# Two strip transposes of the first batch held behind loads of the second batch's v, in a fused attention and mixer kernel

## The chip, the cores and the metric

The kernel runs on one core of one Trainium2 chip. The metric is the device time of one execution in microseconds, as the median of several runs. A profile of one more execution shows what each engine did: PE (TensorE), DVE (VectorE), ACT (ScalarE), POOL (GpSimd) and SP (SyncE, which here only issues DMAs).

## The reference

There are 8 batches of 3136 rows. An attention without softmax is gated by `u`, and a mixer with a low-rank term and two channel matrices follows.

```python
scores = (1.0 / S) * np.matmul(z, z.transpose(0, 2, 1))      # z: 8 x 3136 x 64
attn = np.maximum(scores, 0.0) ** 2
x = u * np.matmul(attn, v)                                   # u, v: 8 x 3136 x 256
h = x.transpose(0, 2, 1) @ U @ V                             # U: 3136 x 32, V: 32 x 3136
y = x + h.transpose(0, 2, 1)
out = y + np.maximum(y @ w_ch1, 0.0) @ w_ch2                 # 256 -> 1024 -> 256
```

## The kernel before

Every order is written out by hand: each engine runs its instructions in the order in which the program names them, and the scheduler moves nothing.

**Tiles.** The 3136 rows of a batch are 25 tiles of 128, numbered 0 to 24, of which the last is half full. The attention matrix is symmetric, so for each row tile `j` only 13 of the 25 blocks are computed: the panel `A[j]` holds the blocks (j, j) to (j, j+12), counted round the 25. PE multiplies the parts of z into PSUM (L359), ACT applies the ReLU and the scale (L372), DVE squares (L374). The 12 blocks that are missing for output `o` are the mirror images of blocks that lie in `A[o]`: one DMA transpose of `A[o][:, 128:]` writes them into a tile called a strip (function `turn`, L394). A strip is 128 x 12 x 128 in bf16, and its DMA is issued by SP. The pool holds seven strips. Output `o` is the sum over 25 blocks times v (function `half`, L472), 13 from panels and 12 from its strip. Outputs are accumulated in pairs; `close_pair` takes a pair out of PSUM (L486, L487), multiplies it by u (L502) and so frees the pair's tile of u. As the last step of the first output of a pair, block 24 of both outputs is taken together, which reads the strips of both.

**Order of the first batch.** Outputs are taken in the order 12, 13, ..., 24, 0, ..., 11. "Output 4" and "output 8" in that order are blocks 16 (`LEAD`) and 20 (`LEAD + NG`); the text calls their strips strip 16 and strip 20. `start_up` does outputs 12 to 15, then 16 to 19 together, since little of A exists yet; it calls `turn` for the strips 16, 17, 18, 19, 20, 21 and 22 in this order. The main loop starts with output 20 (`attend_steps`), whose list `js` says in which order its blocks are taken: for output 20 five blocks from panels, then its strip, then the other eight panel blocks. Strips 23, 24, 0 and so on follow from the main loop. SP issues the transposes in this order, and a transpose that waits holds all that follow it.

**The loads.** POOL issues the loads of v, u, z and the weights in program order, and the few POOL instructions between them wait in the same line. v of the next batch comes in nine pieces: `V_PARTS` is (0,3), (3,6), (6,9), (9,12), (12,15) and so on in tiles, of 192 KB each in SBUF. `start_up` issues the pieces 0 to 2 of batch 1 behind the loads of the first weight matrix, U and V (L306). Pieces 3 and 4 are issued later, behind a one-column copy on POOL from strip 19 into a tile `mark` that nothing reads (L869): the copy makes POOL wait until strip 19 has landed. Then come the loads of u for outputs 20 and 22 (L456), each of which also waits until DVE has freed its buffer, and the two halves of the last, short piece of v (L309).

Of the kernel before, what the change touches and what calls it, by code (L numbers as in the profile page):

```python
# [42 lines left out]
def kernel(  # L43
# [11 lines left out]
    nc = tc.nc  # L55

    B, S, D = u.shape
# [13 lines left out]
    NB = HALF + 1  # L71
    FIRST = HALF
    AHEAD = 4
    LEAD = FIRST + AHEAD
    NG = 4
# [20 lines left out]
    mark = persist.tile([P, 1], BF16, name="mark")  # L96
# [29 lines left out]
    v_both = [persist.tile([P, NT, D], BF16, name=f"v{k}") for k in range(2)]  # L126
# [5 lines left out]
    def turns(i):  # L132
        return (FIRST + i) % NT
# [168 lines left out]
    def load_v(b, part):  # L302
        t0, t1 = part
        v_bf = v_both[b % 2]
        if t0 < NF:
            pool_dma(out=v_bf[:, t0:t1, :], in_=rows(v[b])[:, t0:t1, :])  # L306
        else:
            for r in halves:
                pool_dma(out=v_bf[r, NF, :], in_=v[b, NF * P :, :])  # L309

    V_PARTS = [(t, t + 3) for t in range(0, NF, 3)] + [(NF, NT)]
# [36 lines left out]


    strips = {}  # L350

    def score(b, parts):

        ps = pair_psum()
        zT = zT_of(b)
        zT_flat = zT.rearrange("p t c -> p (t c)")
        at = (min(b, 1), 0)
        for k, (j, c, n, _) in enumerate(parts):
            mm(  # L359
                out=ps[:, k, :n],  # L360
                lhsT=zT[halves[k], j + at[k], :],
                rhs=zT_flat[halves[k], c + at[k] * P : c + at[k] * P + n],
                start=True,
                stop=True,
            )
        if parts[0][3] is parts[-1][3]:
            n = parts[0][2]
            todo = [(parts[0][3], ps[:, :, :n] if len(parts) == 2 else ps[:, 0, :n])]
        else:
            todo = [(part[3], ps[:, k, : part[2]]) for k, part in enumerate(parts)]  # L370
        for dst, src in todo:
            nc.scalar.activation(out=dst, in_=src, func=AF.Relu, scale=sc)  # L372
        for dst, _ in todo:
            nc.vector.tensor_tensor(out=dst, in0=dst, in1=dst, op=ALU.mult)  # L374
# [16 lines left out]

    def turn(b, o):
        strip = strip_pool.tile([P, HALF, P], BF16, name="strip")
        transpose(out=strip, in_=A[o][:, P:])  # L394
        strips[b, o] = strip

# [40 lines left out]
    def turned(b, j):  # L437
        steps = score_steps(b, j)
        s = steps.pop()
        return steps + [lambda: (s(), turn(b, j))]  # L440
# [5 lines left out]
    def pair_of(o):  # L446
        first = 0 if o < FIRST else FIRST
        stop = FIRST if o < FIRST else NT
        t0 = o - (o - first) % 2
        return t0, min(2, stop - t0)  # L450

    def load_u(b, o):
        t0, n = pair_of(o)
        u_sb = u_pool.tile([P, 2, D], FP32, name="u_sb")
        if o < NF:
            pool_dma(out=u_sb[:, :n, :], in_=rows(u[b])[:, t0 : t0 + n, :])  # L456
        else:
            for r in halves:
                pool_dma(out=u_sb[r, 0, :], in_=u[b, NF * P :, :])
        u_tiles[b, t0] = u_sb  # L460

    def open_pair(b, o):
        acc[pair_of(o)[0]] = sets[opened[0] % 2]
        opened[0] += 1

    def block(b, o, j):
        k = (o - j) % NT
        return A[j][:, k * P : (k + 1) * P] if k <= HALF else strips[b, o][:, NT - 1 - k, :]

    def half(b, o, j, h, w, start, stop, **kw):  # L470
        t0, _ = pair_of(o)
        mm(  # L472
            out=acc[t0][h][:, (o - t0) * D : (o - t0 + 1) * D],
            lhsT=w[halves[h]],
            rhs=v_both[b % 2][halves[h], j, :],
            start=start,
            stop=stop,
            **kw,
        )

    def close_pair(b, o):
        t0, n = pair_of(o)
        banks, u_sb = acc.pop(t0), u_tiles.pop((b, t0))
        w = n * D
        both = both_pool.tile([P, 512], FP32, name="both")
        nc.scalar.copy(out=both[:, :w], in_=banks[1][:, :w])  # L486
        nc.vector.tensor_tensor(  # L487
            out=both[:, :w], in0=banks[0][:, :w], in1=both[:, :w], op=ALU.add
        )
        if o == NF and b == 0:  # L490

            for bank in banks:
                for r in range(2):
                    q = both[halves[r], :w]
                    nc.vector.tensor_tensor(out=q, in0=bank[halves[1 - r], :w], in1=q, op=ALU.add)
        elif o == NF:
            for r in range(2):
                nc.scalar.copy(out=both[halves[r], w : 2 * w], in_=both[halves[1 - r], :w])
            nc.vector.tensor_tensor(
                out=both[:, :w], in0=both[:, :w], in1=both[:, w : 2 * w], op=ALU.add  # L500
            )
        nc.vector.tensor_tensor(  # L502
            out=x_at(b, t0, n),
            in0=split(both[:, :w]),
            in1=u_sb[:, :n, :].rearrange("p t (a c) -> p t a c", c=P),
            op=ALU.mult,
        )

    def quarter(b, j, n, h):

        c = n % 2
        mm(  # L512
            out=acc[NF][h][halves[c], :D],
            lhsT=block(b, NF, j)[halves[h], halves[c]],
            rhs=v_both[b % 2][halves[h], j, :],
            start=(n < 2),
            stop=(n == (NT - 2 if c else NT - 1 - 2 * h)),
        )

    def after(b, o):  # L520

        t0, n = pair_of(o)
        i = place(t0) + n
        return (b, turns(i)) if i < NT else (b + 1, turns(0))

    def attend_steps(b, o):
        t0, n = pair_of(o)
        last = t0 + n - 1
        js = [(o - k) % NT if k < NB else (o + k - HALF) % NT for k in range(NT)]
        if b == 0 and o == LEAD + NG:  # L530
            js = js[: NG + 1] + js[NB:] + js[NG + 1 : NB]
        js.remove(NF)

        def step(i):
            if i == 0 and o == t0:
                open_pair(b, o)
            if i == 16 and o == t0 and after(b, o)[0] < B:
                load_u(*after(b, o))
            if o == NF:
                if i < NT - 1 and i % 2:  # L540
                    for n in (i - 1, i):
                        for h in range(2):
                            quarter(b, js[n], n, h)
                elif i == NT - 1:
                    quarter(b, NF, i, 0)
            elif i < NT - 1:
                w = block(b, o, js[i])
                end = i == NT - 2
                half(b, o, js[i], 0, w, i == 0, end and o > t0)
                half(b, o, js[i], 1, w, i == 0 and o == t0, end)  # L550
            elif o == t0:
                half(b, o, NF, 0, block(b, o, NF), False, True)
                if o < last:
                    half(b, o + 1, NF, 1, block(b, o + 1, NF), True, False)
            if i == NT - 1 and o == last:
                close_pair(b, o)

        return [lambda i=i: step(i) for i in range(NT)]
# [209 lines left out]
    def start_up():  # L768
# [4 lines left out]
            out=eye,  # L773
            in_=eye,
# [91 lines left out]
        ]  # L866
        run(_merge(nxt[2:], own))
        if B > 1:
            nc.gpsimd.tensor_copy(out=mark, in_=strips[0, LEAD + NG - 1][:, 0, :1])  # L869
            for part in V_PARTS[3:5]:  # L870
                load_v(1, part)
        rest = [
# [4 lines left out]
        for i, pair in enumerate(pairs):  # L877
            if i + 2 < len(pairs):
                make_stored(pairs[i + 2], LEAD)
            else:  # L880
                more.pop(0)()
            use_stored(pair, outs)
            if i == len(pairs) - 1:
                turn(0, LEAD + NG)
        tail = []
        for o in outs:
            js = [(o + 1 + i) % NT for i in range(HALF)]
# [49 lines left out]

    fetches, second_w, puts, copies = weight_steps()
    panel = start_up()
    puts = dict(zip((17, 18, 19, 20, 16, 21, NT), puts + copies))  # L940
    late = []
# [6 lines left out]
    for b in range(B):  # L948
# [8 lines left out]
        for i in range(begin, NT):  # L957
            o = turns(i)
# [7 lines left out]
            if more:  # L966
# [14 lines left out]
                if b == 0 and i == 15:  # L981
                    mirror_z((0, FIRST))
                    extend_z(b + 1)
            main = attend_steps(b, o)
            if b and i in ahead:
                at = 17 if (i + (i > FIRST)) % 2 == 0 else 12 if i == 7 else 9 if i == 3 else 10
# [39 lines left out]
    b = B - 1  # L1026
# [46 lines left out]
```

## Time and profile before

| | us |
|---|---|
| median of 3 runs (993.81 to 998.08) | 995.57 |
| profiled execution, its own time | 995.98 |
| span of its instructions | 994.3 |
| PE busy | 978.9 (98%) |
| ACT busy | 615.5 (62%) |
| DVE busy | 552.7 (56%) |
| POOL busy | 169.5 (17%) |

Of the span, PE's busy time leaves 15.4 us. The granted clock is 1.00 throughout. On the chain of work that ended last, PE has 95% and DMA 2%. The DMA engines are shared by the transposes (queue q1, 96.14 MB in packets of mostly 256 bytes) and the loads and stores of POOL (queue q0, 66.28 MB). A row of a DMA names where it was issued and how long the issue took; "to landing" is the time from the start of the issue until its semaphore was complete. In the list of idle times of an engine, the operation behind the arrow is the one whose end released it.

### The profile page before, as it was taken

How to read it: one execution, taken by the hardware profiler on the slowest of the kernel's cores; microseconds unless marked ns; L12 is line 12 of the kernel's file. 1: busy time of each engine (PE TensorE's matmuls, PEld its weight loads, DVE VectorE, ACT ScalarE, POOL GpSimd, SP SyncE). 2: the span in 40 equal slices, each digit the busy share in tenths (PEclk: the TensorE clock that was granted, in tenths of full speed). 3: DMA queues.
4: the chain of work that ended last, by engine and by line, in shares of the span. 5: the costliest groups of instructions: out<-in, count | busy, mean ns of one | idle time of the engine just before them, and what ended most of it. 6: DMA issues, size and time to landing. Idle time of an engine off the chain costs nothing.

```text
span 994.3 us, 31019 instructions
## 1 busy us (share of the span) xinstructions
PE 978.9 (98%) x13632; PEld 815.5 (82%) x13672; DVE 552.7 (56%) x1025; ACT 615.5 (62%) x845; POOL 169.5 (17%) x317
## 2 busy tenths in 40 slices
PE   8899999999999999999999999999999999999998
PEld 6778878888788888788887888878888788788876
DVE  6779845567346574364653655546546466352342
ACT  8878764766647575475755757467574676643154
POOL 5111111112121111212112121121211201111000
PEclk9999999999999999999999999999999999999999
DMA  9999999899899998998989989889989796595443
GB/s 180 163 192 209 181 155 202 174 184 174 142 196 175 168 178 151 181 179 169 168 163 172 180 166 169 162 171 186 159 165 185 164 192 125 129 191 122 83 107 101
DMA packets 399976, 164.42 MB, mean 165 GB/s; under 512 B 375568, under 2 KB 384464, under 8 KB 399840
## 3 DMA queue, kind: packets, MB, share of 16 engines
q1 hardware_dynamic: 371520, 96.14, 61.5%
q0 software_dynamic: 28320, 66.28, 28.9%
q8 instruction: 107, 1.75, 0.8%
q14 instruction: 29, 0.24, 0.1%
HBM read 61.88 MB, written 25.69 MB: 88 GB/s over the span
## 4 chain that ended last, share of the span: by engine, by line
PE 95%; DMA 2%; DVE 1%; ACT 1%; issue 0%; POOL 0%; DVEq 0%; POOLq 0%
PE ps L472 51%; PE ps L701 17%; PE ps L654 17%; PE ps L359 7%; DMA strip<-A 1%; PE ps L622 1%; PE ps L512 1%; DMA v<-in_v_dram 1%; ACT A L372 1%; PE ps L567 1%; DVE A L374 0%; DMA out_dram<-o_sb 0%; DVE both L487 0%; ACT both L486 0%; DVE x_bf L502 0%
## 5 line engine op out<-in xcount | busy, mean ns | idle before, releaser
L372 ACT ACTIVATE A<-ps 128x832 bf16<-128x832 f32 (+9 forms) x481 | 358.4, 764 | 141.0 <-PE ps L359 135.6
L472 PE MATMUL ps<-v,A 64*128 64x256 bf16 x4988 | 341.2, 269 | 1.6 <-DVE A L374 1.1
L374 DVE TENSOR_TENSOR A<-A 128x832 bf16<-128x832 bf16 (+9 forms) x481 | 243.5, 523 | 135.4 <-ACT A L372 133.1
L472 PE MATMUL ps<-v,strip 64*128 64x256 bf16 x4420 | 310.3, 269 | 3.8 <-DMA strip<-A 3.0
L472 PEld LDWEIGHTS <-A 64*128 64x128 bf16 x4988 | 252.7, 94 | 40.0 <-issue 7.0
L672 ACT ACTIVATE relu_bf<-ps 128x1024 bf16<-128x1024 f32 (+2 forms) x208 | 188.3, 909 | 150.5 <-PE ps L654 144.7
L472 PEld LDWEIGHTS <-strip 64*128 64x128 bf16 x4420 | 227.6, 94 | 35.0 <-DMA strip<-A 4.6
L701 PE MATMUL ps<-w_bf,relu_bf 128*128 128x256 bf16 (+1 forms) x1600 | 201.4, 273 | 0.4
L654 PE MATMUL ps<-ut,w_bf 128*128 128x512 bf16 (+2 forms) x856 | 198.1, 353 | 1.7
L701 PEld LDWEIGHTS <-relu_bf 128*128 128x128 bf16 (+1 forms) x1600 | 153.0, 98 | 40.3 <-issue 4.9
L719 DVE TENSOR_TENSOR o_sb<-ps,x_bf 128x512 f32<-128x512 f32 (+2 forms) x81 | 54.8, 678 | 171.1 <-PE ps L701 166.1
L654 PEld LDWEIGHTS <-w_bf 128*128 128x128 bf16 x896 | 117.9, 144 | 37.4 <-issue 6.7
L359 PE MATMUL ps<-zT 64*128 64x416 bf16 (+8 forms) x812 | 134.8, 312 | 0.0
L456 POOL DMA_DIRECT2D u_sb<-in_u_dram x96 | 53.1, 554 | 444.4 <-DVE x_bf L502 426.3
L486 ACT COPY both<-ps 128x512 f32<-128x512 f32 (+1 forms) x104 | 59.0, 568 | 70.1 <-PE ps L472 64.0
L487 DVE TENSOR_TENSOR both<-ps,both 128x512 f32<-128x512 f32 (+1 forms) x104 | 69.3, 666 | 30.8 <-ACT both L486 30.2
L502 DVE TENSOR_TENSOR x_bf<-both,u_sb 128x512 bf16<-128x512 f32 (+1 forms) x104 | 69.8, 672 | 3.7
L636 DVE TENSOR_TENSOR x_bf<-ps,x_bf 128x512 bf16<-128x512 f32 (+1 forms) x112 | 65.5, 626 | 11.3 <-PE ps L622 11.2
L732 POOL DMA_DIRECT2D out_dram<-o_sb x66 | 36.1, 546 | 186.4 <-DVE o_sb L719 174.5
L359 PEld LDWEIGHTS <-zT 64*128 64x128 bf16 x812 | 46.3, 94 | 3.6
L719 DVE TENSOR_TENSOR both<-ps,x_bf 128x512 f32<-128x512 f32 (+1 forms) x24 | 15.0, 623 | 57.3 <-PE ps L701 57.3
L306 POOL DMA_DIRECT2D v<-in_v_dram x61 | 33.7, 556 | 3.9 <-issue 2.7
(65 smaller groups left out, 242.8 us busy)
## 6 DMA issues: line engine op xcount, KB each, us to landing
u_sb<-in_u_dram POOLq DMA_DIRECT2D x96, 256.0 KB, 4.2
out_dram<-o_sb POOLq DMA_DIRECT2D x66, 256.0 KB, 2.9
v<-in_v_dram POOLq DMA_DIRECT2D x57, 192.0 KB, 4.5
out_dram<-both POOLq DMA_DIRECT2D x18, 256.0 KB, 2.5
strip<-A SPq DMA_TRANSPOSE x194, 5.5
out_dram<-o_sb SPq DMA_DIRECT2D x11, 256.0 KB, 2.0
z_c<-in_z_dram POOLq DMA_DIRECT2D x7, 384.0 KB, 7.0
w_bf<-in_moe_w_ch_dram POOLq DMA_DIRECT2D x2, 512.0 KB, 7.6
```

Source lines behind the costliest of these rows:

```text
L359: mm(out=ps[:, k, :n], lhsT=zT[halves[k], j + at[k], :], rhs=zT_flat[halves[k], c + at[k] * P : c + at[k] * P + n], start=True, stop=True,)
L372: nc.scalar.activation(out=dst, in_=src, func=AF.Relu, scale=sc)
L374: nc.vector.tensor_tensor(out=dst, in0=dst, in1=dst, op=ALU.mult)
L472: mm(out=acc[t0][h][:, (o - t0) * D : (o - t0 + 1) * D], lhsT=w[halves[h]], rhs=v_both[b % 2][halves[h], j, :], start=start, stop=stop, **kw,)
L486: nc.scalar.copy(out=both[:, :w], in_=banks[1][:, :w])
L487: nc.vector.tensor_tensor(out=both[:, :w], in0=banks[0][:, :w], in1=both[:, :w], op=ALU.add)
L502: nc.vector.tensor_tensor(out=x_at(b, t0, n), in0=split(both[:, :w]), in1=u_sb[:, :n, :].rearrange("p t (a c) -> p t a c", c=P), op=ALU.mult,)
L636: nc.vector.tensor_tensor(out=q, in0=split(ps[h][:, : len(ks) * D]), in1=q, op=ALU.add)
L654: mm(out=ps[i][:, :w] if apart else ps[:, i, :w], lhsT=w1_at[:, db, hp + i, :], rhs=uT[c][:, db, len(chunks[c]) * P - w :], start=(db == 0 ...
L672: nc.scalar.activation(out=relus[c][:, hp : hp + 2, :w], in_=ps[:, :, :w], func=AF.Relu)
L701: mm(out=ps[r, k * D : (k + 1) * D], lhsT=relus[c][:, ht, q : q + (TAIL if two else P)], rhs=w2_bf[:, ht, :], start=(ht < 1 + two), stop=( ...
L719: nc.vector.tensor_tensor(out=o_sb[:p].rearrange("p t (a c) -> p t a c", c=P), in0=split(ps[:p, k0 * D : (k + 1) * D]), in1=x_at(b, t, nk) ...
```

## The change

Two lines make a POOL instruction write one column of a strip from a piece of v of batch 1 before the strip's transpose is issued. The transpose writes the same column, so it waits for POOL, and POOL waits for the piece to land: strip 16 waits for piece 2, strip 20 for piece 4. The copy into `mark`, ahead of pieces 3 and 4, reads strip 18 in place of strip 19. Output 20 takes nine panel blocks ahead of its strip in place of five, and four behind it in place of eight.

```diff
+    behind = {(0, LEAD): V_PARTS[2], (0, LEAD + NG): V_PARTS[4]} if B > 1 else {}
...
     def turn(b, o):
         strip = strip_pool.tile([P, HALF, P], BF16, name="strip")
+        if (b, o) in behind:
+            t = behind[b, o][1] - 1
+            nc.gpsimd.tensor_copy(out=strip[:, 0, :1], in_=v_both[1][:, t, :1])
         transpose(out=strip, in_=A[o][:, P:])
         strips[b, o] = strip
...
         if b == 0 and o == LEAD + NG:
-            js = js[: NG + 1] + js[NB:] + js[NG + 1 : NB]
+            js = js[: NG + 5] + js[NB:] + js[NG + 5 : NB]
...
         if B > 1:
-            nc.gpsimd.tensor_copy(out=mark, in_=strips[0, LEAD + NG - 1][:, 0, :1])
+            nc.gpsimd.tensor_copy(out=mark, in_=strips[0, LEAD + NG - 2][:, 0, :1])
             for part in V_PARTS[3:5]:
                 load_v(1, part)
```

No other instruction is added, removed or moved: POOL runs 2 more, PE and SP the same number as before.

## The prediction

> **What bounds the kernel now.** I read the page first (busy times), then the busy time by windows, the waits of one stretch, and last the timelines of PE, POOL and SP in that stretch.
>
> ```profile
> PE 978.9 (98%) x13632; PEld 815.5 (82%) x13672; DVE 552.7 (56%) x1025; ACT 615.5 (62%) x845; POOL 169.5 (17%) x317
> ```
>
> PE is the bound: a change pays only where PE stands still. Between 40 and 64 us the windows (PE busy is the second number of a row) say where that is:
>
> ```profile
> 40.00:44.00 4.00, 3.86 (x64) 3.30 (x61) 3.97 (x11) 4.00 (x11) 0.61 (x2) 1.00 1.08 125
> 44.00:48.00 4.00, 2.20 (x39) 1.83 (x36) 2.67 (x6) 1.83 (x3) 1.60 (x3) 1.00 1.30 150
> 52.00:56.00 4.00, 2.56 (x44) 1.95 (x39) 2.96 (x6) 2.84 (x5) 1.06 (x2) 1.00 1.20 177
> 56.00:60.00 4.00, 3.19 (x56) 2.63 (x52) 1.50 (x5) 2.35 (x5) 0.00 (x0) 1.00 1.14 253
> ```
>
> PE's own timeline names three stops, the bracket being the idle time and its releaser:
>
> ```profile
> 42.63 0.74 PE L472 MATMUL ps<-v,A 64*128 64x256 bf16 x10
> 43.18 0.41 PE L472 MATMUL ps<-v,strip 64*128 64x256 bf16 x4
> 47.71 0.28 PE L472 MATMUL ps<-v,strip 64*128 64x256 bf16 x1 [1.80 <-DMA strip<-A]
> 54.64 0.72 PE L472 MATMUL ps<-v,strip 64*128 64x256 bf16 x10 [1.23 <-DMA strip<-A]
> 57.15 0.28 PE L472 MATMUL ps<-v,strip 64*128 64x256 bf16 x1 [0.81 <-DVE z_c L246]
> ```
>
> By the order of the strips these are the first reads of strips 21, 22 and 23 (at 57.15 the named DVE row is a coincidence: strip 23, issued at 47.16 with 9.9 us to landing, landed at 57.1). Together **3.84 us**, 0.39% of the time. After 60 us no wait of PE reaches 0.2 us. So the change can win at most about 4 us, and anything beyond 0.5% (4.98 us, about what a measurement of this kernel can tell from no change) could only be a loss.
>
> Why the strips are late is in the timelines of SP and POOL (start, length of the issue):
>
> ```profile
> 20.22 6.33 SPq L394 DMA_TRANSPOSE strip<-A  x1
> 37.07 1.44 SPq L394 DMA_TRANSPOSE strip<-A  x1
> 38.95 1.86 SPq L394 DMA_TRANSPOSE strip<-A  x1
> 40.92 6.05 SPq L394 DMA_TRANSPOSE strip<-A  x1
> ```
>
> ```profile
> 38.75 0.22 POOL L869 COPY mark<-strip 128x1 bf16<-128x1 bf16 x1 [9.62 <-DMA strip<-A]
> 38.98 1.08 POOL L306 DMA_DIRECT2D v<-in_v_dram  x2
> 42.20 0.55 POOL L456 DMA_DIRECT2D u_sb<-in_u_dram  x1 [2.14 <-DVE x_bf L502]
> 45.95 0.54 POOL L456 DMA_DIRECT2D u_sb<-in_u_dram  x1 [3.20 <-DVE x_bf L502]
> ```
>
> The SP rows are strips 16, 20, 21 and 22, which took 11.0, 3.8, 8.7 and 13.7 us to landing. Strip 20 ran alone. Strip 21 ran beside pieces 3 and 4 of v (4.9 and 7.4 us to landing; lone pieces, at 141, 255 and 300 us, take 3.7), strip 22 beside two loads of u (10.8 and 8.2 us). Transposes and loads that share the DMA engines slow each other.
>
> **The change part by part.**
>
> *Hold of strip 16.* Its panel is squared at 20.2. Piece 2 of v, issued at 20.09 with 9.9 to landing, lands at 30.0, but its end is shared with strip 16, which will no longer be there. Pieces 0 to 2 were moving at some 190 KB/us before the strip's packets came; I estimate a landing at 27.5, with 30.0 as the late bound. Then the copy (0.22, as the `mark` row), and strip 16 starts at 27.8. Behind the waiting copy POOL holds the loads of u for 16 and 18 (issued at 26.75 and 28.58, used by DVE from 41.2 on, so a delay of 1 to 3 us is covered). SP holds strips 17 to 19. What a strip takes when a load of u is issued within half a microsecond of it, with no other DMA around, is seen later in the kernel:
>
> ```profile
> 448.09 1.49 SPq L394 DMA_TRANSPOSE strip<-A  x1
> DMA to landing us min/median/max: 5.2/5.2/5.2
> 448.10 0.54 POOL L456 DMA_DIRECT2D u_sb<-in_u_dram  x1 [6.07 <-DVE x_bf L502]
> ```
>
> Four more such meetings, at 442, 454, 805 and 811 us, took 5.4, 6.4, 5.4 and 6.6; I take 5.4. Strip 16 then lands at 33.2, and 17 and 18 behind it at about 2.3 each (17 to 18 took 2.5, 18 to 19 1.2, 19 to 20 2.2) at 35.5 and 37.8. Before, they landed at 31.2, 35.0 and 37.5. PE first reads strip 16 at 35.6 and the next ones about 1.8 apart (92 products in 7.06 us), at 37.3 and 39.1. The hold is covered: cost 0. If piece 2 still lands at 30.0, strip 16 lands at 35.6 and everything below is up to 2.5 later (the late bound).
>
> *Mark at strip 18.* Strip 18 landed at 37.5 (7.0 after its start at 30.51), strip 19 at 38.7. POOL issued piece 3 0.28 after strip 19; now it does so at 37.8, 1.2 earlier, and piece 4 at 38.3. No strip moves beside them any more, since 20 waits: piece 3 lands at 37.8 + 3.7 = 41.5 and piece 4 1.05 behind it (as pieces 1 and 2 before), at 42.6. If the second is not queued behind the first, 38.3 + 3.7 = 42.0.
>
> *Hold of strip 20.* This is where it bites. Strip 20 could start at 37.07; now it starts at 42.6 + 0.3 = 42.9. POOL's next instruction, the load of u for output 20 (42.20 before), goes out at the same 42.9; DVE needs it some 10 us later, which covers the 0.7. So strip 20 starts into exactly the meeting above: 5.4 to landing, at **48.3** (46.7 if it runs as alone, 3.8; 51.6 if like strip 21 before, 8.7).
>
> *Order of output 20.* Before, PE first reads strip 20 at 43.18. Four more panel blocks are 8 products of 0.055 (0.44) and one pair of score products (0.18) moves ahead: first read at 43.8. DVE squared these four blocks between 41.8 and 43.3, each at least 0.4 ahead of its new read, so the order itself costs nothing. New wait: 48.3 - 43.8 = **4.5** (2.9 to 7.8).
>
> *Strips 21 to 23.* Strip 21 was needed at 45.9 (47.71 - 1.80), 2.7 after the first read of strip 20; with the moved blocks 2.1 after. At about 2.3 behind strip 20 it costs 0.2 to 0.3. Strip 22 is needed 5.7 later (47.71 to 53.41), strip 23 1.7 after that; with nothing but u beside them they come 2 to 3 apart, and the stall itself moves their need by 2 us. Their waits, 1.23 and 0.81, go. Strip 23's panel is squared later, since its scores are issued behind strip 20's products, but it has about 2 us to spare.
>
> *Sum.* Waits removed 1.80 + 1.23 + 0.81 = 3.84; waits added 4.5 + 0.3 = 4.8. Net +1.0 on the profiled 995.98 (span 994.3 and 1.7 around it): 996.9; on the median, which is 0.4 lower, **996.5**.
>
> The Trainium skill, DMA: Bandwidth & Descriptors, in the section on the anatomy of a SWDGE DMA, gives 2.0 us plus bytes over 436 KB/us: 2.5 us for a piece by estimate. Piece 4 would land at 40.8 and the sum would be -0.8; the lone pieces' 3.7 us say otherwise, and the row is used. The same page's Rules for kernel authors speak against the change: "A transpose next to ordinary DMAs needs nothing". As a rule of safety no run here tests it; as one of time, strip 21's 8.7 us against 3.8 do not agree with it.
>
> **The rivals.**
>
> *Clean hand-over (24%).* The transpose moves its packets before u's begin, or the two share the engines without loss. For it: three strips at 216, 579 and 821 us whose load of u came 1.5 us behind them took 3.7, as alone. Against: here POOL issues u at once. Strip 20 lands at 46.0 to 46.7, wait 2.2 to 2.9, strip 21 0.3: -1.3 to -0.6, so 994.6, and 993.0 if an earlier strip 18 is added.
>
> *Crowding (20%), the slow side.* Strips 20, 21 and 22, all ready by 40.6, are now released in one go beside the loads of u for 20 and 22, the very mix in which strip 22 and those loads took 8 to 13 us. Strip 20 takes 8.7: lands at 51.6, wait 7.8 + 0.3, net +4.3: 999.8. It decides against the kernel from a landing of strip 20 past 47.3, where the new waits equal the old, and by over 0.5% from 52.3; if the late bound of the first hold is added to 51.6, it is past that.
>
> *The first hold is late (6%).* Piece 2 lands at 30.0 as before, strip 18 at 40, `mark` and all behind it 2.5 later, PE's need a little later too by new stops at strips 17 and 18: +3 to +4, 999.
>
> That a hold changes nothing can be left out for strip 20: the piece it waits for landed at 46.95, strip 20 at 40.9.
>
> **How the numbers follow.** The exchange of waits as summed gets 50%, with its own range 995 to 998. The range 993.0 to 1001.0 takes in clean hand-over and most of crowding, with about 1 us for the median's scatter. Faster by over 0.5% would need more than all the waits that there are: 4%, scatter alone. Slower by over 0.5% needs crowding on top of a late first hold or a further stop: 18%. Within 0.5%: 78%.
>
> **What would show it.** In the changed profile: strip 16 starting near 28; pieces 3 and 4 issued near 37.8 and landing by 42.6; strip 20's start near 42.9 beside u's; one stop of PE of some 4.5 us at output 20's strip near 44 to 48, and none at strips 22 and 23. Wrong if strips 16 to 19 stop PE, if strip 20 lands before 46 or after 50, or if stops appear after 60 us.

## The result and the profile after

| | before | changed |
|---|---|---|
| median of 20 executions each, us | 996.0 | 1000.4 |
| profiled execution, us | 995.98 | 1005.07 |
| its span, us | 994.3 | 1003.4 |
| its PE busy, us | 978.9 | 981.2 |

The changed kernel is slower: the ratio is 1.0049, with a 95% interval of 1.0034 to 1.0064. That is 4.4 us between the medians, where +1.0 was forecast. The time lies inside the range, and just inside the half per cent, which the interval reaches past. The twenty executions fall in two groups, ten between 998.2 and 999.1 and nine between 1001.7 and 1005.1, with one at 1025.1 beyond both. The profiled one is the last of the second group; no profile shows the first.

The busy times of the changed kernel:

```profile
PE 981.2 (98%) x13632; PEld 816.4 (81%) x13672; DVE 552.9 (55%) x1025; ACT 614.9 (61%) x845; POOL 170.3 (17%) x319
```

PE has the same instructions and is busy 2.3 us longer: some of them ran slower. (0.7 us of it lies in the first 13 us, ahead of all that the change touches.) The windows show where. PE busy is the second number of a row; the third from the end is the granted clock.

```profile
44.00:48.00 4.00, 0.73 (x13) 0.39 (x8) 2.82 (x7) 1.72 (x5) 1.43 (x4) 1.00 0.09 17
48.00:52.00 4.00, 0.00 (x0) 0.00 (x0) 0.00 (x0) 0.00 (x0) 0.92 (x2) 0.50 1.21 151
52.00:56.00 4.00, 0.88 (x10) 0.76 (x12) 0.00 (x0) 0.00 (x0) 0.00 (x0) 0.50 1.06 202
56.00:60.00 4.00, 4.00 (x54) 3.43 (x52) 0.59 (x1) 1.39 (x2) 0.00 (x0) 0.72 0.34 77
```

PE stood still, and its clock fell to 0.50 and stayed there for a while after the work had returned. PE's timeline gives the stops of more than 0.3 us after 30 us:

```profile
38.07 0.61 PE L476 MATMUL ps<-v,strip 64*128 64x256 bf16 x8 [0.60 <-DMA strip<-A]
55.12 2.32 PE L476 MATMUL ps<-v,strip 64*128 64x256 bf16 x20 [10.38 <-DMA strip<-A]
83.27 1.48 PE L476 MATMUL ps<-v,strip 64*128 64x256 bf16 x24 [0.51 <-DMA strip<-A]
```

The second is output 20's first read of its strip: 20 products in 2.32 us, which at full clock take 1.27. The stops at strips 21, 22 and 23 are gone. POOL's and SP's timelines tell how strip 20 came to be late:

```profile
39.30 0.19 POOL L873 COPY mark<-strip 128x1 bf16<-128x1 bf16 x1 [9.41 <-DMA strip<-A]
39.53 1.08 POOL L306 DMA_DIRECT2D v<-in_v_dram  x2
46.24 0.20 POOL L397 COPY strip<-v 128x1 bf16<-128x1 bf16 x1 [5.63 <-DMA v<-in_v_dram]
46.77 1.08 POOL L460 DMA_DIRECT2D u_sb<-in_u_dram  x2 [0.33 <-DVE x_bf L506]
```

```profile
46.47 1.44 SPq L398 DMA_TRANSPOSE strip<-A  x1
```

The view of the strips in that microsecond, which holds this transpose alone, adds its time to landing:

```profile
DMA to landing us min/median/max: 8.5/8.5/8.5
```

The mark was released at 39.3 in place of 37.8 as forecast, piece 4 took 6.1 us to land (46.2), and strip 20 started together with both loads of u, with the two halves of the last piece of v close behind them (POOL, 47.84), and took 8.5.

**The account of this execution.** Stops now 0.60 + 10.38 + 0.51 = 11.49, before 3.84: +7.65. From the first product of strip 20 to the row that next waits for ACT (63.88) PE took 8.76 us; two kernels further down do the same work at full clock in 7.26. The clock thus cost 1.50. Together 9.15; measured 1005.07 - 995.98 = 9.09. From 85 us to the end PE runs a steady 9.3 us behind the profile before, so the whole loss lies ahead of that.

### The profile page after: what moved, and what is told of

The parts are those of the page before. It is cut to its first block, busy times and chain, and to the rows that moved or that the text cites. A ratio compares the mean times of both kernels' runs of the same rounds, so it can differ in the third digit from the quotient of the medians.

```text
span 1003.4 us, 31025 instructions
## 1 busy us (share of the span) xinstructions
PE 981.2 (98%) x13632; PEld 816.4 (81%) x13672; DVE 552.9 (55%) x1025; ACT 614.9 (61%) x845; POOL 170.3 (17%) x319
## 4 chain that ended last, share of the span: by engine, by line
PE 94%; DMA 2%; ACT 1%; issue 1%; DVE 1%; POOL 0%; POOLq 0%; DVEq 0%
PE ps L476 50%; PE ps L705 17%; PE ps L658 17%; PE ps L360 7%; DMA strip<-A 2%; PE ps L626 1%; PE ps L516 1%; ACT A L373 1%; PE ps L571 1%; DVE A L375 0%; PE ps L269 0%; PE ps L285 0%; DVE both L491 0%; ACT both L490 0%; DVE x_bf L506 0%
```

## The experiments

Each ratio is against executions of the kernel before, taken alongside.

| run | ratio (95% interval) | its profile: strip 20 start, to landing | longest stop at strips 20 to 23 |
|---|---|---|---|
| changed kernel | 1.0049 (1.0034 to 1.0064) | 46.47, 8.5 | 10.38 |
| changed kernel again | 1.0102 (1.0068 to 1.0136) | 44.66, 4.9 | 4.39 |
| hold of 16 alone | 1.0000 (0.9976 to 1.0024) | as before | 3.62 |
| no hold of 16 | 1.0027 (1.0001 to 1.0054) | 39.64, 4.9 | 0.80 |
| no holds | 1.0006 (0.9979 to 1.0034) | as before | 3.69 |
| loads of u behind strip 20 | 1.0013 (0.9994 to 1.0031) | 42.84, 3.8 | 2.89 |
| the same again | 1.0040 (1.0018 to 1.0062) | 42.88, 3.8 | 2.90 |
| the same, PE kept busy | 1.0014 (0.9994 to 1.0034) | 45.65, 3.8 | 2.96 |
| the same again | 1.0022 (1.0001 to 1.0042) | 45.27, 3.8 | 0.54 |

**Which hold makes the loss.** The first hold alone:

```diff
-    behind = {(0, LEAD): V_PARTS[2], (0, LEAD + NG): V_PARTS[4]} if B > 1 else {}
+    behind = {(0, LEAD): V_PARTS[2]} if B > 1 else {}
```

(mark and the order of output 20 as before.)

> Only the hold of strip 16 behind piece 2 is kept; mark, order and strip 20 are as before. If the hold of strip 20 makes the loss: within 1.5 us of the kernel before (994.5 to 997.5), no stop of PE over 3 us, clock 1.00. If the first hold makes it, by shifting strips 17 to 19, mark and all behind it by about 2 us: 998 to 1000, with the stops at strips 21 and 22 grown from 1.8 and 1.2 to 3 and more.

It costs nothing that can be measured, though two things expected of the profile were missed: its stop is over 3 us, and the clock fell to 0.50 for 3.4 us behind it. In its profile strip 16 starts at 26.70, not 20.2, and yet lands at 31.6 (31.2 before): the hold only takes away the stretch in which it crawled beside the loads. PE's one long stop is that of the kernel before, at strip 21:

```profile
49.20 0.28 PE L476 MATMUL ps<-v,strip 64*128 64x256 bf16 x1 [3.62 <-DMA strip<-A]
```

The second hold without the first (`behind` with the key `(0, LEAD + NG)` alone):

> The whole change without the hold of strip 16. If the hold of strip 20 makes the loss by itself: one stop of PE of 6 us or more at strip 20, clock under 1.00, 998 to 1001. If the late first hold was needed on top: strip 18 lands at 37.5, piece 4 by 43, the stop is 4 us or less and the time 995 to 997.

Its executions spread from 992.4 to 1005.1 with a median of 998.1, and the one that was profiled is one of the quickest (992.74), with the clock at 1.00: mark was released at 34.6, strip 20 started at 39.64, and the stop was small.

```profile
44.68 1.27 PE L476 MATMUL ps<-v,strip 64*128 64x256 bf16 x20 [0.80 <-DMA strip<-A]
```

Here piece 4 landed early (39.3), and the stops at strips 20 and 21 come to 1.08 in place of 3.84. That this wins is not shown: the quickest executions of the kernel before on that chip, from 992.27 on, are as quick. In nine of the twelve executions the clock was under 1.00, and these took 996.6 to 1005.1; this profile cannot say where they lost it. The expected stop of 6 us or more was not seen, though the median fell where that theory put it.

Neither hold (`behind = {}`), mark at strip 18 and the new order kept:

> Neither hold; mark at strip 18 and the new order of output 20 stay. If the holds are the loss: 994 to 997, stops at strips 21 and 22 of 1 to 4 us in sum, as before. If issuing the pieces one strip sooner, beside strips 19 to 21, costs by itself: 998 or more, with strip 20 landing past 44 and a stop there.

The loss is gone (the two intervals just touch), so it comes with the holds, and of the two with that of strip 20; whether the first adds to it is open, since the intervals of the whole change and of this hold alone overlap. The new order costs nothing measurable by itself. Issuing the pieces sooner was hardly tried: in this profile strip 18 landed late, and the pieces went out at 39.03, against 38.98 before.

```profile
38.63 0.46 POOL L873 COPY mark<-strip 128x1 bf16<-128x1 bf16 x1 [10.14 <-DMA strip<-A]
39.03 1.07 POOL L306 DMA_DIRECT2D v<-in_v_dram  x2
```

The stop is back at strip 21, again with 3.4 us of half clock behind it:

```profile
48.98 0.39 PE L476 MATMUL ps<-v,strip 64*128 64x256 bf16 x1 [3.69 <-DMA strip<-A]
```

**Crowding or late start.** The whole change, with the loads of u for 20 and 22 behind strip 20, and so, since POOL keeps its order, the two halves of the last piece of v as well:

```diff
                 if o == outs[1]:
+                    nc.gpsimd.tensor_copy(out=mark, in_=strips[0, LEAD + NG][:, 0, :1])
                     load_u(0, LEAD + NG)
```

> The whole change, and the loads of u for outputs 20 and 22 wait, by a one-column copy on POOL, until strip 20 has landed. If crowding by these loads stretches strip 20: it lands 3.8 to 4.2 us after its start in place of 8.5, the stop at strip 20 shrinks by 4 us and the time goes to 995 to 997. If the late start alone counts: strip 20 still lands 7 us or more after its start, and the time stays at 998 to 1002.

> The kernel whose loads of u wait for strip 20, once more, as the partner of the next one on the same chip. If it repeats: a stop of 2.5 to 5 us at strip 20, clock 0.998 in most executions, 0.1 to 0.4% over the kernel before.

In both profiles strip 20 lands 3.8 us after its start, against 8.5 where both loads of u and the halves of v went beside it: these loads together do stretch it. The 4.9 beside one load of u, in the second profile of the changed kernel, does not show it, since strip 20 has taken as long with no load beside it (4.8, further down). What is left is the late start. The profiled execution of the first of the two runs took 1014.66, with stops of up to 6.95 us long behind strip 20, after 120 us. From the second of the two runs: SP's timeline, the strips' time to landing in the window of that row, PE's timeline, and the busy times of the window behind the stop.

```profile
42.88 1.44 SPq L398 DMA_TRANSPOSE strip<-A  x1
```

```profile
DMA to landing us min/median/max: 3.8/3.8/3.8
```

```profile
46.78 1.67 PE L476 MATMUL ps<-v,strip 64*128 64x256 bf16 x20 [2.90 <-DMA strip<-A]
55.71 0.30 PE L360 MATMUL ps<-relu_bf 64*128 64x288 bf16 x2 [0.22 <-ACT A L373]
```

```profile
47.50:50.90 3.40, 3.40 (x35) 2.85 (x32) 0.59 (x1) 0.86 (x1) 1.98 (x4) 0.50 1.07 218
```

The stop is 2.90, less than the 3.84 of the kernel before, and still the kernel is no faster than that one, and in the second run slower. The last row shows a part of the reason: for 3.4 us behind the stop PE works at half clock. From 46.78 to 55.71 it takes 8.93 us, 1.67 more than at full clock, as the next run shows. Stop and clock make 4.57, 0.7 over the 3.84. The profiled execution (996.29) is the quickest of its run; where the others, up to 1000.64, lost the rest is not shown. The ratios, 1.0013 and 1.0040, lie under the changed kernel's two, but the interval of the second overlaps that of its first: that crowding costs time is shown in the strip's flight, not settled in the whole.

**What the clock costs.** The same kernel with twelve added products of 128x512 ahead of output 20's strip, some 2.6 us in which PE would stand still; nobody reads their result:

```diff
+            if b == 0 and o == LEAD + NG and i == NG + 5:
+                ps = pair_psum()
+                for n in range(12):
+                    mm(out=ps[:, n % 2, :], lhsT=zT_first[:, 0, :], rhs=..., start=True, stop=True)
```

> The kernel whose loads of u wait for strip 20, with 12 added products of 128x512 (some 2.6 us, their result is read by nobody) ahead of output 20's strip, inside the stop of 2.9 us. If the idle time makes the clock fall to half for 3.4 us behind the stop, and that costs 1.7 us: the clock is 1.00 in the executions and the time 995 to 996, against 997.25 without the products. If the clock does not matter here: 997 to 998, or later by what the products add.

> The same with the 12 unread products ahead of output 20's strip. If the half-speed stretch behind the stop costs time: 1 to 2 us less than its partner, with a clock of 1.00. If the products only take up the wait and the clock costs nothing that can be seen: within 0.7 us of its partner.

The clock was 1.00 in 13 of the 18 executions; without the products it was under 1.00 in every execution. In the first of the two profiles strip 20 came so late that PE still stood for 2.96 us behind the products, and yet the clock stayed at 1.00. In the profile that shares a chip with its partner, PE's timeline and the window behind the stop:

```profile
49.17 1.27 PE L476 MATMUL ps<-v,strip 64*128 64x256 bf16 x20 [0.54 <-DMA strip<-A]
56.43 0.30 PE L360 MATMUL ps<-relu_bf 64*128 64x288 bf16 x2 [0.22 <-ACT A L373]
```

```profile
49.10:52.50 3.40, 3.33 (x60) 3.24 (x62) 0.59 (x1) 1.34 (x2) 2.33 (x5) 1.00 1.19 211
```

The same work takes 7.26 us, so that one half-speed stretch of 3.4 us costs 8.93 - 7.26 = 1.67. On that chip the medians of six executions are 996.57 with the products and 999.23 without. The intervals of the two ratios overlap, and the first pair of runs, on two chips, shows no gain (1.0014 with, 1.0013 without): the price of a stretch is measured, its gain in the total is not settled.

**The changed kernel once more.**

> The changed kernel once more, for a second profile. If the loss is the crowded hand-over at strip 20: the executions fall in two groups near 998.5 and 1002 to 1005, the granted clock is under 1.00 in all of them, and in this profile too one stop of 4 us or more stands at strip 20, with a half-speed stretch of the clock behind it. If the first profile was an odd one: no stop over 3 us and a clock of 1.00.

On another chip it was 1.0102, clearly more than the first 1.0049. Its profiled execution took 1012.86 us:

```profile
37.01 0.61 PE L476 MATMUL ps<-v,strip 64*128 64x256 bf16 x8 [1.51 <-DMA strip<-A]
49.71 2.32 PE L476 MATMUL ps<-v,strip 64*128 64x256 bf16 x20 [4.39 <-DMA strip<-A]
150.26 1.93 PE L658 MATMUL ps<-ut,w_bf 128*128 128x512 bf16 x4 [10.38 <-DMA ut<-x_bf]
```

Piece 4 landed at 44.1 here, only one load of u went out with strip 20, and the stop at strip 20 is the size of the forecast. With the stops of 0.16 and 0.38 at 74 and 78 us the early stops are 6.44, which is 2.60 over the 3.84 of before; the clock adds 1.57 (8.83 to the ACT row, minus 7.26). That makes 4.2, close to the difference of the first medians. The third row is another matter: a stop at the transposes of x in the second batch, which four of the other kernels' profiles show too (up to 4.2 us, between 127 and 148 us), two of them without a hold of strip 20. Whether this change makes it more frequent was not tried, and all six executions took over 1002, so why the two measurements differ stays open.

**The first hold beside the loads of u.** The kernel with u behind strip 20, less the hold of strip 16:

> The kernel whose loads of u wait for strip 20, without the hold of strip 16. If the first hold adds to the loss by landing strip 18 and so pieces 3 and 4 late: strip 20 starts 1 to 3 us sooner, the stop falls under 2 us, the time to 993 to 996. If the first hold is free: 996.5 to 998 as with it.

The profiled execution (994.71) did as expected: strip 20 starts at 39.64 in place of 42.88, and the stop is 0.71. It also shows what a strip takes with no load beside it. From SP's timeline, the strips' time to landing in the window of that row, and POOL's timeline:

```profile
39.64 1.44 SPq L398 DMA_TRANSPOSE strip<-A  x1
```

```profile
DMA to landing us min/median/max: 4.8/4.8/4.8
```

```profile
39.36 0.26 POOL L397 COPY strip<-v 128x1 bf16<-128x1 bf16 x1 [3.65 <-DMA v<-in_v_dram]
44.58 0.19 POOL L898 COPY mark<-strip 128x1 bf16<-128x1 bf16 x1 [4.96 <-DMA strip<-A]
45.14 0.55 POOL L460 DMA_DIRECT2D u_sb<-in_u_dram  x1 [0.38 <-DVE both L491]
```

POOL issued no load between piece 4, whose landing released strip 20, and 45.14, and the strip took 4.8 us, not 3.8. Why is open.

The whole did not do as expected: 1.0027 (1.0004 to 1.0051), from 992.0 to 1003.1 in the executions compared. With the hold they lay between 995.1 and 998.2 on one chip and between 996.3 and 1000.6 on another, at ratios on both sides of this one (1.0013 and 1.0040). So what the first hold does to the whole here is not settled. The bad executions were not profiled, so their cause is open.

**Away with what collides.** The kernel before, without mark, its pieces 3 and 4 moved into the main loop (steps 12 and 15; then steps 15 and 17; then the latter with the hold of strip 16):

```diff
-            nc.gpsimd.tensor_copy(out=mark, in_=strips[0, LEAD + NG - 1][:, 0, :1])
-            for part in V_PARTS[3:5]:
-                load_v(1, part)
...
-        v_at = dict(zip((17, 20, 22, 10), V_PARTS[5:]))
+        v_at = dict(zip((17, 20, 22, 10, 12, 15), V_PARTS[5:] + V_PARTS[3:5]))
```

> The kernel before, without mark, and with pieces 3 and 4 issued in the main loop of the first batch at its steps 12 and 15 in place of ahead of output 20. If the pieces beside the strips 21 and 22 make the 3.84 us of stops of the kernel before: stops under 1 us in sum, clock 1.00, 991.5 to 993. If the loads of u alone are enough to make strips 21 and 22 late: 995 to 997 as before, with the stop at strip 22.

> The kernel before with pieces 3 and 4 issued at the steps 15 and 17 of the first batch (and pieces 5 to 7 one step later each, at 19, 21 and 23), without mark. If the pieces beside strips 21 and 22 cause the stops there, and nothing else takes their place: 0.1 to 0.4% under the kernel before, clock 1.00 in nearly all executions. If later strips stop in their place, or batch 1 waits for its v: no gain.

> The same with strip 16 held behind piece 2. If the first hold keeps strips 16 to 19 in a steadier order: times closer together than its partner, and as low. If it costs by itself: a stop of 0.5 to 1.5 us at strip 16 or 17, and 0.5 to 2 us more than its partner.

The ratios are 1.0002 (0.9978 to 1.0027), 1.0005 (0.9956 to 1.0054) and 0.9996 (0.9955 to 1.0037): no gain is shown. The second and third have six executions each, which spread from 990.8 to 1023.2 and from 991.2 to 1008.4. In all three profiles the stops at strips 21 to 23 are gone, as expected if the pieces cause them; in the third only this one is left, at strip 20, in an execution of 992.79 us:

```profile
44.26 0.39 PE L476 MATMUL ps<-v,strip 64*128 64x256 bf16 x4 [0.69 <-DMA strip<-A]
```

None is at strips 16 or 17, where the first hold was expected to show if it cost by itself; whether the times are steadier with it cannot be told from six executions. The profiles of the first two have new stops: 1.35 at a strip at 67.9 us, 2.40 on a piece of v that landed too late for batch 1, at 101 us, 2.48 at a strip at 114 us, and the stops at the transposes of x.

## Why the prediction was right or wrong

**The bound was right.** Nothing could be won beyond 3.84 us, and the direction came out as forecast. The waits at strips 21 to 23 went as forecast. The price at strip 20 was too low, and the rival called crowding (+4.3, a flight of 8.7) is what the first profile shows in the flight, though not in the total: there it came on top of a late start.

**That the time fell in the range is in part luck.** The +4.4 is about what the rival forecast, and four times the +1.0 of the sum. In the second measurement the median is 1004.15 and the ratio 1.0102, outside the range and beyond the half per cent. By the prediction's own signs the mechanism was wrong in the first profile: PE stopped at strip 17 (0.60), strip 20 landed at 55.0, after 50, and a stop stands past 60 us (0.51 at 83).

**The step at strip 20 was right by itself.** In the second run with the loads behind strip 20, where mark came in time (37.4), its figures came out: start 42.88 (42.9 in the working), landing 46.7 (46.7 for a lone strip), a stop of 2.90 (2.9). What failed are the terms that feed it, and one behind it.

**Strip 18, and with it mark.** Put at 37.8, it landed at 39.2 in both profiles of the changed kernel. Two terms of the first hold failed. Strip 16 started at 28.75 and 29.03, not 27.8, since piece 2 landed later than estimated. And its flight beside u was put at 5.4, from five meetings with one load of u each, where here two loads went out in one go behind POOL's copy; it took 6.8 and 7.8. (In the run with the first hold alone the two loads went out 1.5 us apart, and the flight was 4.9.) Strips 17 and 18 caught up a part of this. The cover of the first hold had been worked out as whole; it left stops of 0.60 and 1.51.

**Piece 4.** Put at 42.6, it landed at 46.2 and 44.1: 1.7 of it from the late mark, the rest from its own flight (6.1 and 4.2, where 4.3 was summed). A hold passes every such delay on to the strip and so to PE.

**Strip 20's flight.** 5.4 was the row for one load of u; with one it took 4.9, with both and the halves of v 8.5. That the late release lets the second load of u catch up stood in the rival's text but not in the sum.

**The clock was missing from the sum**, 1.5 to 1.6 us in both profiles. The trace of before held only stops of up to 1.80 here and a clock of 1.00, so a stop of 4.5 us should have had a price of its own beyond its length. One trace was too few for this: the clock was 0.998 or less in 35 of 76 executions of the kernel before that were run alongside the experiments, against all 26 of the changed kernel. One stretch of 3.4 us at half clock is what makes 0.998. So the kernel before pays for such a stretch too, in nearly half of its executions.

**The rule against the change.** The rule of the Trainium skill (DMA: Bandwidth & Descriptors, Rules for kernel authors) that a transpose beside ordinary DMAs needs nothing gave the right sign, but not by its letter: strip 20 took 3.8 to 4.8 us with no load beside it and 8.5 beside two loads of u and the halves of v, so they do slow each other. Here the wait costs more than it saves.

## What to carry to other kernels

Before holding a transfer back behind another, give the hold its own row: the release's latest time, what else the same release lets go, and how long PE then stands. Where PE is the bound, one long stop can cost more than several short ones of the same sum, because the clock may fall behind it (here 2.90 us cost 4.57, and the 3.84 of the profile before cost no clock). Idle products that took up part of such a stop kept the clock up here.

## What the runs showed of the hardware

The granted clock falls to half in stretches of 3.4 us or a multiple of it. A stop of 2.90 us brought one, and cost 1.67 us of slow work behind it; the stop of 10.38 brought 10.2 us of it, most of it while PE stood still anyway. The stops of 1.80 and 1.23 in the kernel before brought none. The length of a stop does not decide alone: in the first run with the added products a stop of 2.96 us brought no such stretch, and one of 2.00 us, at 131 to 133 us, did. Counted in steps of 3.4 us back from where the clock changes, the stop of 2.90 left PE 0.72 us of work in the step ahead of the change, while the stop of 2.96 was split over two steps with 1.81 and 2.03 us of work. That the share of work within such a step decides fits these two, and is not tested further. The Trainium skill, TensorE: Matmul & The Clock Gate, in its Part 1, says that the clock is set by free-running activity windows of 3413 ns, and halves after an idle one. The length agrees; that a stop of 2.90, shorter than a window, is enough goes beyond that sentence.

Pieces 3 and 4 of v, 192 KB each and with no strip issued beside them, took from 3.7 to 6.1 us to land in the two profiles of the changed kernel. Where PE is made to wait for such a DMA, its scatter reaches PE: strip 20 started between 39.64 and 46.47 in the profiles with its hold.
